# Two h units moved between the first columns, five relus split over two engines, one more tile's y from mixed blocks

## The chip, the cores and the metric

The kernel runs on one core of a Trainium2 chip. The metric is the device time of one execution in microseconds (us), and the median of several executions is quoted. The profile's span, from the first to the last instruction, is about 1.8 us shorter than the time.

The TensorE multiplies matrices and writes to PSUM. VectorE (DVE), ScalarE (ACT) and GpSimd (POOL) do the elementwise work.

## The reference

```python
# u, v: 8 x 3008 x 256; z: 8 x 3008 x 64; w_in: 256 x 2048; w_out: 2048 x 256
scores = np.matmul(z, z.transpose(0, 2, 1)) / 3008
attn = np.maximum(scores, 0.0) ** 2
x = (u * np.matmul(attn, v)).reshape(24064, 256)
h = x @ w_in
g = h * np.cos(h)
y = g @ w_out
```

## The kernel before

The tokens are cut into 48 tiles of up to 512 tokens, six to a batch. Attention is done per tile ("column" of the score matrix). A score group is two 128 x 512 blocks of scores; ScalarE takes the relu, VectorE the square. A column's two output halves (`dh` 0 and 1) gather in two pairs of PSUM banks: the pair `M`, and a pair taken from the three double-bank buffers `E`, which also hold scores and h.

```python
    def emit_score(later=None):
        ...
        r = rpool.tile([P, 2, CW], FP16, name="r")
        nc.scalar.activation(r[:, :, 0:W], e[:, :, 0:W], AF.Relu)
        def square():
            ...
                nc.vector.tensor_tensor(a4, r[:, :, 0:W], r[:, :, 0:W], ALU.mult)
```

At a column's end both pairs must be emptied before the next column may write them. ScalarE copies one bank of a pair, VectorE adds the other:

```python
    def gate_sum(s, b0, b1):
        W = width(s % NC)
        sm = spool.tile([P, CW], FP32, name="sm")
        nc.scalar.copy(sm[:, 0:W], b0[:, 0:W])
        nc.vector.tensor_tensor(sm[:, 0:W], b1[:, 0:W], sm[:, 0:W], ALU.add)
        return sm
```

In columns 0 to 2 no other work is placed that could fill a gap. Key pieces (four steps of 128 keys each) serve one output half and then the other:

```python
    def phase_a_first(s, n, extra={}):
        ...
        acc = [pair, M] if s == 1 else [M, pair]
        last = NB - 1
        steps = [
            (dh, k)
            for I in range(NC)
            for dh in range(2)
            for k in range(4 * I, min(4 * I + 4, last))
        ] + [(2, last)]
        ...
        late_sums.extend(gate_sum(s, *acc[dh]) for dh in range(2))
        hold(late_sums[0][0:1, 0:1])       # POOL waits here for VectorE's sum
        ...
    phase_a_first(0, 12, {4: lambda: turn_late(4), 8: lambda: turn_late(5)})
    phase_a_first(1, 12)
    nc.gpsimd.dma_start(w_out16, moe_w_out.rearrange("(k p) f -> p k f", p=P))
    phase_a_first(2, 14)
    ...
    phase_b(2)
```

An h unit is 4 matmuls of 512 columns into one `E` buffer (8 in a row in a timeline are two units), a cosine on ScalarE, and the product h x cos(h) on VectorE. `phase_b(2)` works off the eight units of tile 0 and the eight of tile 1, with the y of tile 0 between them in eight pieces:

```python
        if s == 2:
            hs = [(0, i) for i in range(8)] + hs
        ...
        if n > 8:
            after = (1, 3, 5, 7, 9, 11, 13, 14)
```

For tiles 1 to 45 y is made from seven products of mixed (added and subtracted) blocks in place of eight; the mixing is done by POOL and VectorE. Tiles 0, 46 and 47 are multiplied directly.

Of the kernel before, what the change touches and what calls it, by code (L numbers as in the profile page):

```python
# [14 lines left out]
def kernel(  # L15
# [9 lines left out]
    nc = tc.nc  # L25
    AF = mybir.ActivationFunctionType
    ALU = mybir.AluOpType
# [151 lines left out]
    turn_slots = {}  # L179
    done_groups = [0]  # L180

    def emit_score(later=None):
        b, J, I, h = groups[done_groups[0]]
        done_groups[0] += 1
        cut = I == J and not (b == 0 and J < 3)
        W = 2 * P if cut and h == 0 else width(J)
        zT = zTs[b]
        e = E[take_e()]
        for t in range(2):
            k = 4 * I + 2 * h + t  # L190
            half = t if h == 0 else 1 - t
            rows = slice(half * H, (half + 1) * H)
            Wt = min(W, (2 * h + t + 1) * P) if cut else W
            nc.tensor.matmul(  # L194
                e[:, t, 0:Wt],
                zT[rows, k * P:(k + 1) * P],
                zT[rows, J * CW:J * CW + Wt],
                start=True,
                stop=True,
            )  # L200
        key = (b, J, I)
        a = new_piece(key) if h == 0 else piece(key)
        r = rpool.tile([P, 2, CW], FP16, name="r")
        nc.scalar.activation(r[:, :, 0:W], e[:, :, 0:W], AF.Relu)  # L204
        def square():
            if I > J:
                a4 = a.rearrange("p (k t j) -> p t k j", k=4, j=P)[:, 2 * h:2 * h + 2, :, :]
                r4 = r.rearrange("p t (k j) -> p t k j", j=P)
                nc.vector.tensor_tensor(a4, r4, r4, ALU.mult)  # L209
            else:  # L210
                a4 = a.rearrange("p (k w) -> p k w", w=CW)[:, 2 * h:2 * h + 2, 0:W]
                nc.vector.tensor_tensor(a4, r[:, :, 0:W], r[:, :, 0:W], ALU.mult)  # L212

        if later is None:
            square()
        else:
            later.append(square)
        if h == 0:
            return
        if cut or (I > J and (b, J, I) not in direct):  # L220
            turns.append(((b, I), key))
            turns.sort(key=lambda t: t[0])
            turn_slots[key] = pieces[key]
            pending[pieces[key]] = "held"
# [122 lines left out]
    def phase_a_first(s, n, extra={}):  # L347
        b, J = s // NC, s % NC
        ea = e_order.pop(0)
        pair = [E[ea][:, 0, :], E[ea][:, 1, :]]  # L350
        acc = [pair, M] if s == 1 else [M, pair]
        last = NB - 1
        steps = [
            (dh, k)
            for I in range(NC)
            for dh in range(2)
            for k in range(4 * I, min(4 * I + 4, last))
        ] + [(2, last)]
        lo, hi = 5 if s == 0 else 2, 42
        at = {}  # L360
        for i in range(n):
            p = lo + (hi - lo) * i // (n - 1)
            at[p] = at.get(p, 0) + 1
        for i, (dh, k) in enumerate(steps):
            if i in extra:
                extra[i]()
            if dh == 2:
                emit_value(b, J, last, 0, 0, acc[0][0], False, True)
                emit_value(b, J, last, 1, 1, acc[1][1], False, True)
            else:  # L370
                for t in range(2):
                    emit_value(
                        b, J, k, t, dh, acc[dh][t], k == 0, k == last - 1 and t != dh
                    )
            if dh > 0 and (k % 4 == 3):
                drop_piece((b, J, k // 4))
                if s > 0:
                    emit_turns((0, 0), 1)
                    if k < 4:
                        turn_u(s)  # L380
                    elif k < 8:
                        for d in range(2):
                            gate_mul(s - 1, d, late_sums.pop(0))
            for _ in range(at.get(i, 0)):
                emit_score(later=squares if s == 0 and i == lo else None)
        if s == 0:
            turn_u(0)
        late_sums.extend(gate_sum(s, *acc[dh]) for dh in range(2))
        hold(late_sums[0][0:1, 0:1])
        load_u(s + 1)  # L390
        e_order.append(ea)
# [24 lines left out]
        )  # L416

    def mixed(m):
        return 1 <= m < NSLOT - 2

    F = NFT // 2
    T = 2 * P
# [38 lines left out]
            )  # L461
        nc.scalar.activation(y_outs[m][0][:, 1, :], acc, AF.Copy, bias=0.0, scale=inv_s2)

    def product(m, n):
        g = gs[m]
        nk, up, low = halves_of(m)
        nk = nk // P
        t = lambda i: w_mix[:, i, :, :]
        left, right = {
            1: (g[:, 0:F, up], w_out16[:, 0:F, 0:P]),  # L470
            2: (g[:, F:, up], w_out16[:, F:, 0:P]),
            3: (s4, w_out16[:, F:, P:D]),
            4: (g[:, F:, low], t(3)),
            5: (s1, t(0)),
            6: (s2, t(1)),
            7: (g[:, 0:F, low], t(2)),
        }[n]
        at = order_y.index(n) + (nk == 1 and n in order_y[4:])
        acc = M[at % 2][:, 0:nk * P]
        for ft in range(F):  # L480
            for k in range(nk):
                nc.tensor.matmul(  # L482
                    acc[:, k * P:(k + 1) * P],
                    left[:, ft, k * P:(k + 1) * P],
                    right[:, ft, :],
                    start=(ft == 0 and k == 0),
                    stop=(ft == F - 1 and k == nk - 1),
                )
        acc = acc.rearrange("p (k d) -> p k d", d=P)
        if n == 5:  # L490
            y_outs[m] = [opool.tile([P, 2, D], FP32, name="o") for i in range(2)]
            y_parts[m] = {}
        c11, c12, c21, c22 = (y_outs[m][i][:, 0:nk, d * P:(d + 1) * P] for i in range(2) for d in range(2))
        parts = y_parts[m]
        add = lambda dst, other: nc.vector.scalar_tensor_tensor(
            dst, acc, inv_s2, other, ALU.mult, ALU.add
        )
        if n in (1, 5, 6):
            parts[n] = ypool.tile([P, 2, P], FP32, name=f"p{n}")[:, 0:nk, :]
        if n in (1, 5):  # L500
            nc.scalar.activation(parts[n], acc, AF.Copy, bias=0.0, scale=inv_s2)
        elif n == 6:
            add(parts[6], parts[1])
            nc.gpsimd.tensor_tensor(c12, parts[6], parts[5], ALU.add)
        elif n == 7:
            add(c21, parts[6])
            nc.gpsimd.tensor_tensor(c22, c21, parts[5], ALU.add)
        elif n == 2:
            add(c11, parts[1])
        elif n == 3:  # L510
            add(c12, c12)
            store_half(m, 0, y_outs[m][0])
        else:
            add(c21, c21)
            store_half(m, 1, y_outs[m][1])

    def y_bank(m, k):
        if m == NSLOT - 1 and k == 3:
            return E[0][:, 0, 0:D]
        return M[k // 2][:, (k % 2) * D:(k % 2 + 1) * D]  # L520

    def y_block(m, ft, k):
        final = m == NSLOT - 1
# [58 lines left out]
    def phase_b(s):  # L582
        y, hs = s - 2, [(s - 1, i) for i in (0, 4, 1, 5, 2, 6, 3, 7)]
        if s == 2:
            hs = [(0, i) for i in range(8)] + hs
        for dh in range(len(late_sums)):
            gate_mul(s, 2 - len(late_sums), late_sums.pop(0), nc.gpsimd)
        if mixed(y):
            ys = [lambda n=n: product(y, n) for n in order_y]
            if mwidth(y) < CW:  # L590
                ys.insert(4, lambda: middle(y))
        else:
            ys = [lambda i=i: emit_y(y, i) for i in range(8)]
            ys[7] = lambda f=ys[7]: (f(), store_y(y))
        n = len(hs)
        if n > 8:
            after = (1, 3, 5, 7, 9, 11, 13, 14)
        elif mixed(y):
            after = (0, 1, 2, 3, 4, 5, 6, 6)
        else:  # L600
            after = (0, 1, 2, 3, 4, 5, 6, 6)
        for i, (m, unit) in enumerate(hs):
            times_c = emit_h(m, unit)
            if not mixed(y):
                times_c()
            for f, place in zip(ys, after):
                if place == i:
                    f()
            if mixed(y):
                times_c()  # L610
            if mixed(m) and unit >= 4:
                mix_early(m, unit - 4)
            if i in (1, 3, 5):
                emit_turns((0, 0), 1)
# [52 lines left out]
    emit_score(later=squares)  # L667
    emit_score(later=squares)
    turn_on_pe(2)
    copy_turned(2)  # L670
    squares.pop(0)()
    squares.pop(0)()
    M = [ppool.tile([P, CW], FP32, name=f"M{i}", tag=f"M{i}") for i in range(2)]

# [25 lines left out]
    phase_a_first(0, 12, {4: lambda: turn_late(4), 8: lambda: turn_late(5)})  # L700
    phase_a_first(1, 12)
    nc.gpsimd.dma_start(w_out16, moe_w_out.rearrange("(k p) f -> p k f", p=P))
    phase_a_first(2, 14)
    assert done_groups[0] == need[3]
    emit_turns((0, 3))
# [63 lines left out]
```

## Time and profile before

| what | value |
|---|---|
| time | 1197.2 us (1196.8 to 1197.6 in 3 runs) |
| span of the profiled run | 1194.3 us |
| TensorE busy | 1184.6 us, 99% |
| first score of column 0 | 5.46 us |
| first h of tile 0 / first y of tile 0 | 52.05 / 55.52 us |
| column 3 begins / h of tile 2 begins | 74.70 / 86.33 us |
| h of tile 47 begins / last y's `E` bank begins | 1168.92 / 1188.06 us |

The landmarks are first starts on the TensorE's timeline. They cut the span into a start that is full of waits (to 86.33 us), a steady part (up to tile 47) and a last stage (to the last `E` bank). The TensorE waits nowhere in the steady part. Of the page's 40 slices, of 30 us each, only the second and the last are below 90% busy; the second row is the granted clock:

```profile
PE   9899999999999999999999999999999999999998
...
PEclk9999999999999999999999999999999999999999
```

### The profile page before, as it was taken

Reading aid. Unit: us, or ns where it says so; the run is one execution under the profiler, and the core shown is the slowest. Engines: PE = TensorE matmul, PEld = TensorE weight load, DVE = VectorE, ACT = ScalarE, POOL = GpSimd, SP = SyncE. Lnnn points to the kernel's source line nnn. Section 1 sums busy time; section 2 is a strip of 40 time slices with the busy share of each in tenths; the row PEclk is TensorE's granted clock in tenths of the full one; section 3 lists DMA queues with packets and bytes.
Section 4 is the critical chain, followed back from the end, with each engine's and each line's share of the span. In section 5 each row is a group of like instructions: output and inputs, shape, how many; then the busy total and the mean of one; then the engine's idle time right before and its main releaser. Section 6 shows DMA issues by size and latency. Waiting matters only on the chain.

```text
span 1194.3 us, 28924 instructions
## 1 busy us (share of the span) xinstructions
PE 1184.6 (99%) x11839; PEld 727.2 (61%) x11839; DVE 1008.6 (84%) x1293; ACT 795.1 (67%) x927; POOL 678.4 (57%) x707
## 2 busy tenths in 40 slices
PE   9899999999999999999999999999999999999998
PEld 4556655665566656566556665666656666665566
DVE  6798988888988898888988889888888888888775
ACT  7866666666766676666766676766766666666454
POOL 3186745557565573665647556476565765545450
PEclk9999999999999999999999999999999999999999
DMA  9999898769995699956999459974798838954301
GB/s 159 172 165 163 121 153 127 118 107 137 139 139 104 114 140 157 128 92 113 150 147 132 91 107 156 169 117 77 121 160 154 122 70 122 183 105 89 65 19 54
DMA packets 479861, 147.98 MB, mean 124 GB/s; under 512 B 404208, under 2 KB 479472, under 8 KB 479728
## 3 DMA queue, kind: packets, MB, share of 16 engines
q1 hardware_dynamic: 380752, 112.93, 54.5%
q0 software_dynamic: 97440, 32.78, 28.1%
q8 instruction: 92, 1.51, 0.5%
q10 hardware_dynamic: 1536, 0.43, 0.2%
q14 instruction: 41, 0.34, 0.1%
HBM read 66.32 MB, written 24.64 MB: 76 GB/s over the span
## 4 chain that ended last, share of the span: by engine, by line
PE 97%; ACT 1%; DVE 1%; issue 1%; ACTq 0%; DVEq 0%
PE E L403 27%; PE M L482 23%; PE M L258 20%; PE E L258 19%; PE E L194 5%; PE M L524 2%; ACT r L204 1%; PE M L459 1%; PE E L654 0%; DVE sm L270 0%; PE E L524 0%; DVE A L209 0%; DVE x L286 0%; DVE g L414 0%; PE M L677 0%
## 5 line engine op out<-in xcount | busy, mean ns | idle before, releaser
L411 ACT ACTIVATE c<-E 128x1024 f16<-128x1024 f32 (+1 forms) x384 | 385.6, 1006 | 218.0 <-PE E L403 214.8
L414 DVE SCALAR_TENSOR_TENSOR g<-E,c 128x1024 f16<-128x1024 f32 (+1 forms) x384 | 458.9, 1197 | 66.7 <-ACT c L411 65.7
L204 ACT ACTIVATE r<-E 128x512 f16<-128x512 f32 (+1 forms) x342 | 327.8, 967 | 114.1 <-PE E L194 108.4
L258 PEld LDWEIGHTS <-v 64*128 64x128 f16 x4512 | 246.8, 94 | 232.4 <-issue 20.6
L403 PE MATMUL E<-x,w_in 128*128 128x512 f16 (+1 forms) x1408 | 353.8, 375 | 0.0
L432 POOL TENSOR_TENSOR s<-g 128x512 f16<-128x512 f16 (+1 forms) x180 | 202.9, 1127 | 185.4 <-DVE g L414 138.9
L258 PE MATMUL M<-A,v 64*128 64x512 f16 (+1 forms) x2256 | 284.9, 372 | 2.1 <-ACT sm L269 1.2
L258 PE MATMUL E<-A,v 64*128 64x512 f16 (+1 forms) x2256 | 279.4, 372 | 0.0
L433 POOL TENSOR_TENSOR g<-g 128x512 f16<-128x512 f16 (+1 forms) x180 | 214.2, 1190 | 14.1
L403 PEld LDWEIGHTS <-w_in 128*128 128x128 f16 x1536 | 133.4, 98 | 108.6 <-issue 19.1
L482 PEld LDWEIGHTS <-g 128*128 128x128 f16 x2752 | 168.6, 98 | 39.8
L209 DVE TENSOR_TENSOR A<-r 128x1024 f16<-128x1024 f16 x240 | 173.3, 734 | 15.1 <-ACT r L204 14.3
L286 POOL TENSOR_TENSOR x<-sm,uT 128x512 f16<-128x512 f32 (+1 forms) x43 | 48.5, 1130 | 214.1 <-DVE sm L270 213.9
L482 PEld LDWEIGHTS <-s 128*128 128x128 f16 x2064 | 126.6, 98 | 30.6
L194 PE MATMUL E<-zT 64*128 64x512 f16 (+4 forms) x684 | 130.0, 356 | 0.5 <-ACT zT L647 0.3
L439 DVE TENSOR_TENSOR s<-s,g 128x1024 f16<-128x1024 f16 (+1 forms) x90 | 98.5, 1094 | 2.1 <-POOL s L432 2.1
L482 PE MATMUL M<-w_out,g 128*128 128x128 f16 x1376 | 91.5, 219 | 0.0
L482 PE MATMUL M<-w_mix,g 128*128 128x128 f16 x1376 | 91.5, 219 | 0.0
L482 PE MATMUL M<-w_mix,s 128*128 128x128 f16 x1376 | 91.5, 219 | 0.0
L212 DVE TENSOR_TENSOR A<-r 128x512 f16<-128x512 f16 (+1 forms) x102 | 80.7, 792 | 10.2 <-ACT r L204 9.4
L194 PEld LDWEIGHTS <-zT 64*128 64x128 f16 x684 | 39.3, 94 | 36.7 <-issue 2.2
L441 DVE TENSOR_TENSOR s<-g,s 128x1024 f16<-128x1024 f16 (+1 forms) x90 | 59.4, 662 | 0.0
(58 smaller groups left out, 657.6 us busy)
## 6 DMA issues: line engine op xcount, KB each, us to landing
out_dram<-o SPq DMA_DIRECT2D x87, 256.0 KB, 2.2
v<-in_v_dram POOLq DMA_DIRECT2D x40, 256.0 KB, 9.2
u<-in_u_dram POOLq DMA_DIRECT2D x40, 256.0 KB, 4.8
A<-A SPq DMA_TRANSPOSE x252, 5.2
z<-in_z_dram POOLq DMA_DIRECT2D x14, 192.0 KB, 10.6
z<-in_z_dram POOLq DMA_DIRECT2D x14, 176.0 KB, 6.3
v<-in_v_dram POOLq DMA_DIRECT2D x8, 192.0 KB, 12.0
u<-in_u_dram POOLq DMA_DIRECT2D x8, 192.0 KB, 4.0
```

The costliest lines, as they stand in the source:

```text
L194: nc.tensor.matmul(e[:, t, 0:Wt], zT[rows, k * P:(k + 1) * P], zT[rows, J * CW:J * CW + Wt], start=True, stop=True,)
L204: nc.scalar.activation(r[:, :, 0:W], e[:, :, 0:W], AF.Relu)
L209: nc.vector.tensor_tensor(a4, r4, r4, ALU.mult)
L212: nc.vector.tensor_tensor(a4, r[:, :, 0:W], r[:, :, 0:W], ALU.mult)
L258: nc.tensor.matmul(bank[:, 0:width(J)], vs[b, k // 4][t * H:(t + 1) * H, k % 4, dh * P:(dh + 1) * P], value_rhs(b, J, k, t), start=start, ...
L403: nc.tensor.matmul(e[:, f, 0:W], w_in16[:, k, ft * P:(ft + 1) * P], x[:, k, 0:W], start=(k == 0), stop=(k == 1),)
L411: nc.scalar.activation(c[:, :, 0:W], e[:, :, 0:W], AF.Sin, bias=half_pi, scale=inv_s2)
L414: return lambda: nc.vector.scalar_tensor_tensor(gs[m][:, 2 * i:2 * i + 2, 0:W], e[:, :, 0:W], 1.0, c[:, :, 0:W], ALU.mult, ALU.mult)
L432: nc.gpsimd.tensor_tensor(s1[:, f, 0:n], g[:, f, low], g[:, lower, low], ALU.add)
L433: nc.gpsimd.tensor_tensor(g[:, f, low], g[:, f, up], g[:, f, low], ALU.subtract)
L439: nc.vector.tensor_tensor(s2[:, f, 0:n], s1[:, f, 0:n], g[:, f, up], ALU.subtract)
L482: nc.tensor.matmul(acc[:, k * P:(k + 1) * P], left[:, ft, k * P:(k + 1) * P], right[:, ft, :], start=(ft == 0 and k == 0), stop=(ft == F - ...
```

## The change

The author wants to close the TensorE's gaps at the start, and to save a little at the end, in four parts.

1. **Piece order.** In columns 1 and 2 each output half takes two key pieces at a time, so the second pair of banks is needed 8 steps after the column's start and not 4.
2. **Moved h units.** Two h units of tile 0 fill the gap between columns 1 and 2. Fourteen units remain after column 2, and the pieces of y move forward among them.
3. **Tile 46** gets its y from mixed blocks; tile 47 uses the `M` banks in the other order.
4. **Shared relus.** In groups 0, 14, 15, 26 and 27 (the first, and the last two of columns 0 and 1) ScalarE takes one half of the relu and VectorE the other. Group 0's square is also done in two halves, and earlier.

```diff
+    shared_groups = {0, 14, 15, 26, 27}
...
-        nc.scalar.activation(r[:, :, 0:W], e[:, :, 0:W], AF.Relu)
+        shared = done in shared_groups
+        n = 1 if shared else 2
+        nc.scalar.activation(r[:, 0:n, 0:W], e[:, 0:n, 0:W], AF.Relu)
+        if shared:
+            nc.vector.tensor_scalar(r[:, 1, 0:W], e[:, 1, 0:W], 0.0, None, ALU.max)
...
+        run = 1 if s == 0 else 2
...
-            for I in range(NC)
+            for I in range(0, NC, run)
             for dh in range(2)
-            for k in range(4 * I, min(4 * I + 4, last))
+            for k in range(4 * I, min(4 * (I + run), last))
...
-        return 1 <= m < NSLOT - 2
+        return 1 <= m < NSLOT - 1
...
-            hs = [(0, i) for i in range(8)] + hs
+            hs = [(0, i) for i in range(2, 8)] + hs
...
-            ys = [lambda n=n: product(y, n) for n in order_y]
+            late = s == NSLOT
+            ys = [
+                lambda n=n, i=i: product(y, n, i)
+                for i, n in enumerate((1, 5) + order_y[2:] if late else order_y)
+            ]
...
-            after = (1, 3, 5, 7, 9, 11, 13, 14)
+            after = (1, 2, 4, 5, 7, 8, 10, 11)
+        elif s == NSLOT:
+            after = (0, 1, 3, 4, 5, 6, 7)
...
+            if s == NSLOT and i in (1, 3):
+                for c in range(2):
+                    mix_late(y, "s2" if i == 1 else "s4", c)
...
     nc.gpsimd.dma_start(w_out16, moe_w_out.rearrange("(k p) f -> p k f", p=P))
+    for i in range(2):
+        emit_h(0, i)()
     phase_a_first(2, 14)
```

More of the change, by code (lines that the diff above doesn't have):

```diff
@@ L180 @@
     done_groups = [0]
+    shared_groups = {0, 14, 15, 26, 27}
     def emit_score(later=None):
-        b, J, I, h = groups[done_groups[0]]
+        done = done_groups[0]
+        b, J, I, h = groups[done]
         done_groups[0] += 1
@@ L208, in square @@
                 r4 = r.rearrange("p t (k j) -> p t k j", j=P)
-                nc.vector.tensor_tensor(a4, r4, r4, ALU.mult)
             else:
                 a4 = a.rearrange("p (k w) -> p k w", w=CW)[:, 2 * h:2 * h + 2, 0:W]
-                nc.vector.tensor_tensor(a4, r[:, :, 0:W], r[:, :, 0:W], ALU.mult)
+                r4 = r[:, :, 0:W]
+            parts = [slice(0, 1), slice(1, 2)] if done == 0 else [slice(0, 2)]
+            for t in parts:
+                nc.vector.tensor_tensor(a4[:, t], r4[:, t], r4[:, t], ALU.mult)
         if later is None:
@@ L462, in middle, with product @@
         nc.scalar.activation(y_outs[m][0][:, 1, :], acc, AF.Copy, bias=0.0, scale=inv_s2)
-    def product(m, n):
+    def product(m, n, place):
         g = gs[m]
@@ L477, in product @@
         }[n]
-        at = order_y.index(n) + (nk == 1 and n in order_y[4:])
-        acc = M[at % 2][:, 0:nk * P]
+        acc = M[(place + (nk == 1 and place >= 4)) % 2][:, 0:nk * P]
         for ft in range(F):
@@ L489, in product @@
         acc = acc.rearrange("p (k d) -> p k d", d=P)
-        if n == 5:
+        if m not in y_outs:
             y_outs[m] = [opool.tile([P, 2, D], FP32, name="o") for i in range(2)]
@@ L519, in y_bank @@
             return E[0][:, 0, 0:D]
-        return M[k // 2][:, (k % 2) * D:(k % 2 + 1) * D]
+        bank = 1 - k // 2 if m == NSLOT - 1 else k // 2
+        return M[bank][:, (k % 2) * D:(k % 2 + 1) * D]
     def y_block(m, ft, k):
@@ L669 @@
     turn_on_pe(2)
+    squares.pop(0)()
     copy_turned(2)
-    squares.pop(0)()
     squares.pop(0)()
```

## The prediction

> **What bounds the kernel now.** I read the page first (shares and slices), then the waits of the TensorE, then its timeline around those waits, then the timelines of the two engines that ended them, and last the chain that ended last, over the final 20 us.
>
> ```profile
> PE 1184.6 (99%) x11839; PEld 727.2 (61%) x11839; DVE 1008.6 (84%) x1293; ACT 795.1 (67%) x927; POOL 678.4 (57%) x707
> ...
> PE M L524 <- DVE g L414: 1.6, 1, 1.6
> PE M L258 <- ACT sm L269: 1.2, 1, 1.2
> ...
> PE M L258 <- DVE sm L270: 0.9, 2, 0.6
> ```
>
> The TensorE is busy for 1184.6 of 1194.3 us. Its whole list of waits comes to about 5 us, and the timeline puts all of it in the first 56 us: from there to 1190 us it streams without a gap. So the kernel is TensorE-bound, and a change can win only by taking matmul time away or by closing those early gaps. Here are the gaps on the TensorE's timeline.
>
> ```profile
> 23.82 0.38 PE L258 MATMUL M<-A,v 64*128 64x512 f16 x1
> 24.47 0.59 PE L258 MATMUL M<-A,v 64*128 64x512 f16 x3 [0.28 <-DVE sm L270]
> ...
> 36.09 0.38 PE L258 MATMUL E<-A,v 64*128 64x512 f16 x1
> 37.69 0.37 PE L258 MATMUL M<-A,v 64*128 64x512 f16 x1 [1.22 <-ACT sm L269]
> 38.65 0.80 PE L258 MATMUL M<-A,v 64*128 64x512 f16 x5 [0.59 <-DVE sm L270]
> ...
> 52.05 1.90 PE L403 MATMUL E<-x,w_in 128*128 128x512 f16 x8
> 55.52 1.05 PE L524 MATMUL M<-w_out,g 128*128 128x256 f16 x8 [1.58 <-DVE g L414]
> ```
>
> Columns: start, length, engine, line, operation, and in brackets the idle time and what ended it. The printed length of a lone matmul includes its drain (0.38), so I count slots instead: a 512-column matmul, or a pair of half-height ones, takes 0.216 us start to start (16 half-height ones took 1.73 us in the chain). By slots the three gaps are:
> - between columns 0 and 1: 23.82 + 0.216 to 24.47, 0.43 us;
> - between columns 1 and 2: 36.09 + 0.22 to 38.65, less the one matmul in it, 2.1 us;
> - between column 2 and the first tile's y: 52.05 + 8 x 0.216 = 53.78 to 55.52, 1.74 us.
>
> The second gap is a bank pair, M, that ScalarE (copy) and VectorE (sum) must have read before the next column may write it. VectorE does this back to back:
>
> ```profile
> 36.70 0.69 DVE L212 TENSOR_TENSOR A<-r 128x1024 f16<-128x1024 f16 x1 [0.38 <-ACT r L204]
> 37.31 0.68 DVE L270 TENSOR_TENSOR sm<-E,sm 128x512 f32<-128x512 f32 x1
> 37.91 0.68 DVE L270 TENSOR_TENSOR sm<-M,sm 128x512 f32<-128x512 f32 x1
> ```
>
> **What the Trainium skill says.** (1) "VectorE: DVE Perf Modes", section "Why PSUM operands drop a tier": a PSUM operand in fp32 runs at one element per cycle whatever the operation. So a relu of 512 fp32 columns on VectorE costs as much as the two sums above: 0.68 us, next start after 0.60 us. The trace agrees on the sums (512 columns in 0.68 us, 1024 in 1.22 us); no relu on VectorE has run yet. (2) "PSUM — Partial Sum Buffer", section "Specifications (TRN2)": ScalarE and VectorE can read PSUM in parallel when they are in different banks. The two halves of a score tile are 512 fp32 columns each, one bank each, so the shared relu is legal; no run here shows it yet. (3) "TensorE: Matmul & The Clock Gate", section "Wait — 56ns, not 53.3ns?": warm matmuls start 55.6 ns (128 columns) and 215.7 ns (512 columns) apart. The trace agrees: 16 of 128 columns take 0.89 us, 8 of 512 take 1.73 us.
>
> **The change part by part.**
>
> *Moved h units.* Two of the first tile's eight h units (8 matmuls, 1.73 us) move from after column 2 into the second gap. Their x is ready: the gating products ran at 29.2 to 30.5 us. Their weights too: w_in was issued at 14.0 us and landed 11.2 us later. They remove no work, they fill a gap. In the third gap the y of tile 0 then needs VectorE products made long before, not 54.24 to 55.48 us.
>
> *What they collide with.* Each unit also brings a ScalarE cosine (1.0 us) and a VectorE product (1.22 us, next start 1.13), and holds a score buffer until the product has read it. Working through VectorE in program order from the square that starts at 34.60: square to 35.2, half relu to 35.8, square to 36.4, half relu to 37.0, square to 37.6, sum of E to 38.2, sum of M to 38.9, products to 40.0 and 41.2. The TensorE ends column 1 at 36.31, does the h units to 38.04, then waits for M until 38.9, for the first score buffer until 40.0 (it stood at 39.09 in the kernel before) and for the second until 41.2. So it reaches the third score of column 2 near 42.1, against 40.82 before: the 1.73 us are nearly all given back for the moment.
>
> *The credit comes in the third gap.* Column 2 then ends near 53.5 instead of 52.05, but only 12 units follow the first y instead of 14. Two h units fill 53.5 to 55.2, and y of tile 0 can start at about 55.3. That is not free: w_out decides it. It is issued at 39.31 and lands 16.0 us later:
>
> ```profile
> L702 POOL DMA_DIRECT2D w_out<-in_moe_w_out_dram x1: 1159/1159/1159, 39.3 to 39.3; - x1
> ...
> DMA to landing us min/median/max: 16.0/16.0/16.0
> ```
>
> 39.31 + 16.0 = 55.3 us, 0.2 us before its use now. The reader is to see that the wait charged to VectorE hides a transfer that comes only just earlier. From 55.3, 12 units of 0.865 and 8 pieces of y of 0.87 take 17.35 us: the stage ends at 72.65, against 74.77 (the last h of the stage ends there in the chain). Gain 2.1 us.
>
> *Two key pieces per output half, columns 1 and 2.* No matmul is added or removed; the second half of the accumulators is needed 8 steps after the start instead of 4, 0.86 us later. By itself that closes the first gap (0.43 us).
>
> *Shared relus.* Groups 14, 15 and 26, 27 are the last two of columns 0 and 1. ScalarE saves 0.4 us on each (1.02 against 0.60 for 512 columns). But its copy of M starts at 22.99 because the TensorE ended then, and its copy of E at 36.56 likewise, so little is won; VectorE gets 0.60 us more for each, and VectorE has the last word on both banks. At the first seam its sum of E ends near 25.5 instead of 25.02, and the score at 25.07 needs that buffer. I book -0.4 us there, which takes back what the piece order wins. Group 0: four filler matmuls stand in front of the first value matmul anyway; below 0.1 us.
>
> *y of tile 46.* 64 matmuls of 256 columns (8 in 0.87 us: 7.0 us) become 7 products of 16 matmuls of 128 columns (0.89 us each: 6.23 us). That is 0.77 us less for the TensorE. VectorE pays: its 8 products at 1.13, 5 additions at 0.34 and 4 mixing operations at 0.61 make 13.2 us in a stage in which the TensorE now has 8 x 0.865 + 6.23 = 13.15 us. Before, it had 8 x 1.13 = 9 us in 13.9 us:
>
> ```profile
> 1168.22 1.73 PE E L403 x8
> ...
> 1182.98 5.24 PE M L524 x48
> ```
>
> Following both engines by hand, product 6 waits about 0.4 us for the first mix, and the last y starts some 13.7 us after the stage's start instead of 13.9. Gain 0.2 us; the tail after it (4 stores) is as before.
>
> **The sum:** 2.1 + 0.2 + under 0.1 = 2.3 us; 1197.2 - 2.3 = 1194.9 us.
>
> **The rivals.** (a) All gaps close: 0.43 + 2.1 + 1.74 + 0.77 = 5.0 us, 1192.2 us. For it: the four parts aim at exactly these places. Against it: VectorE's list above, and w_out at 55.3 us. (b) The score buffers held by the h units, with VectorE's extra relus, cost as much as the gap: no gain at the start and only the 0.2 us at the end, 1197.0 us. For it: the TensorE is even with the kernel before at 42 us. Against it: the two units need not be done later, and the third gap is 1.74 us of pure waiting. (c) The last stage becomes VectorE-bound, with POOL's mixing slowing it (squares at 77 to 83 us took up to 1.64 us beside POOL instead of 0.69), and loses 0.5 to 1 us: 1195.7 us. (d) w_out lands later, as more transposes compete with it: each us costs a us.
>
> **Range and chances.** From (a) at one end and (b) at the other I take 1193.3 to 1196.8 as eight in ten. A change by 2% is 24 us; all waits and removed work together are 5 us, so within 2% is all but certain (0.985). I leave 0.005 for faster and 0.01 for slower, the latter for an unforeseen stall that repeats in every tile; nothing in the steady tiles changes order.
>
> **What would show it.** Right: the gap between columns 1 and 2 holds 8 matmuls of h; then waits of the TensorE for M (about 0.9 us) and for score buffers that VectorE's h products hold (about 1.2 us); the first y near 55.3 us with w_out or nothing as its releaser; the stage's end near 72.7 us; 7 products beside the h of the last tile, with a short wait for the s2 mix; VectorE near fully busy there. Wrong: y of tile 0 starting well before 55 us (then rival a), the stage ending at 74 us or later (b), the last y starting more than 14.2 us after its stage's start (c), or a new TensorE wait between 75 and 1165 us.

## The result

The changed kernel takes 1194.81 us (1194.51 to 1196.36 in 4 runs), the kernel before 1197.01 us (4 runs in all). All ratios below are the mean time of one kernel's fast runs over that of the other's of the same rounds, so they are not quite the ratio of the medians. Here the ratio is 0.9984, with a 95% interval of 0.9966 to 1.0001: within 2%, and on these runs alone not clear of no change.

The TensorE's list of waits in the profile after (line, who ended the wait, total us, times, longest; three entries of the warm-up and the first scores, 1.2, 0.3 and 0.2 us, which the kernel before has too, are cut):

```profile
PE E L197 <- DVE sm L280: 0.9, 1, 0.9
PE M L268 <- DVE sm L280: 0.6, 1, 0.6
PE E L197 <- DVE r L211: 0.5, 2, 0.3
PE M L268 <- DVE A L222: 0.4, 1, 0.4
PE E L197 <- DVE g L425: 0.3, 1, 0.3
PE M L492 <- POOL s L443: 0.3, 1, 0.3
```

The waits of 1.6 us (for VectorE's h product) and 1.2 us (for ScalarE's copy) are gone. In their place stand smaller ones: the first five hang on VectorE, the sixth is at the end, in tile 46. These are the places on the TensorE's timeline after (start, length, work, and in brackets the idle time and its releaser):

```profile
24.25 0.39 PE L197 MATMUL E<-zT 64*128 64x512 f16 x2 [0.31 <-DVE r L211]
24.47 0.82 PE L268 MATMUL E<-A,v 64*128 64x512 f16 x6
26.18 0.39 PE L197 MATMUL E<-zT 64*128 64x512 f16 x2 [0.89 <-DVE sm L280]
...
37.51 1.90 PE L414 MATMUL E<-x,w_in 128*128 128x512 f16 x8
39.34 0.39 PE L268 MATMUL M<-A,v 64*128 64x512 f16 x1
40.30 0.80 PE L268 MATMUL M<-A,v 64*128 64x512 f16 x5 [0.57 <-DVE sm L280]
...
54.44 1.90 PE L414 MATMUL E<-x,w_in 128*128 128x512 f16 x8
56.31 1.05 PE L535 MATMUL M<-w_out,g 128*128 128x256 f16 x8
```

At 37.51 the two h units fill the old gap between columns 1 and 2. At 54.44 two more lead straight into the first y. But the second score of column 1 starts at 26.18, where the kernel before had it at 25.07, and what it waits for is VectorE's sum. That engine's timeline there:

```profile
22.19 0.68 DVE L211 TENSOR_SCALAR r<-E 128x512 f16<-128x512 f32 x1
22.91 0.69 DVE L222 TENSOR_TENSOR A<-r 128x1024 f16<-128x1024 f16 x1
23.51 0.68 DVE L211 TENSOR_SCALAR r<-E 128x512 f16<-128x512 f32 x1
24.23 0.69 DVE L222 TENSOR_TENSOR A<-r 128x1024 f16<-128x1024 f16 x1
24.84 0.68 DVE L280 TENSOR_TENSOR sm<-M,sm 128x512 f32<-128x512 f32 x1
25.44 0.68 DVE L280 TENSOR_TENSOR sm<-E,sm 128x512 f32<-128x512 f32 x1
```

VectorE works without a pause, the two half relus (L211) stand in front of the sums (L280), and the sum that frees `E` ends at 26.12 us.

The landmarks, with the start of the first score taken off where noted, since that start itself scatters from 5.36 to 5.76 us between profiled runs:

| us | before | after |
|---|---|---|
| first score | 5.46 | 5.37 |
| first score to second score of column 1 | 19.61 | 20.81 |
| first y of tile 0 begins | 55.52 | 56.31 |
| column 3 begins | 74.70 | 73.76 |
| length of column 3 | 11.63 | 11.23 |
| h of tile 2 begins | 86.33 | 84.99 |
| h of tile 2 to h of tile 47 | 1082.59 | 1082.59 |
| h of tile 47 to last `E` bank | 19.14 | 19.08 |
| span | 1194.3 | 1192.9 |

The two profiled runs took 1196.1 and 1194.72 us, so the profile before is of a run 0.9 us faster than its median. The gain in span of 1.4 us is made as follows: the first y starts 0.8 us later, two h units less follow (1.73 us), column 3 is 0.4 us shorter, the last stage 0.06 us. The steady part is the same to 0.01 us.

### The profile page after: what moved, and what is told of

It reads as the page before. It is cut to its first block, busy times and chain, and to the rows that moved or that the text cites. A ratio compares the mean times of both kernels' runs of the same rounds, so it can differ in the third digit from the quotient of the medians.

```text
span 1192.9 us, 29048 instructions
## 1 busy us (share of the span) xinstructions
PE 1183.7 (99%) x11887; PEld 725.8 (61%) x11887; DVE 1015.5 (85%) x1308; ACT 793.1 (66%) x927; POOL 689.7 (58%) x717
## 4 chain that ended last, share of the span: by engine, by line
PE 97%; DVE 1%; ACT 1%; issue 0%; POOL 0%; DVEq 0%; ACTq 0%
PE E L414 27%; PE M L492 23%; PE M L268 20%; PE E L268 19%; PE E L197 5%; PE M L535 1%; ACT r L209 1%; PE M L470 1%; DVE A L222 0%; DVE g L425 0%; DVE r L211 0%; PE E L674 0%; DVE sm L280 0%; PE E L535 0%; POOL s L443 0%
## 5 line engine op out<-in xcount | busy, mean ns | idle before, releaser
L443 POOL TENSOR_TENSOR s<-g 128x512 f16<-128x512 f16 (+1 forms) x184 | 208.0, 1131 | 188.6 <-DVE g L425 138.7
L222 DVE TENSOR_TENSOR A<-r 128x1024 f16<-128x1024 f16 (+2 forms) x343 | 253.3, 750 | 22.5 <-ACT r L209 21.0
L444 POOL TENSOR_TENSOR g<-g 128x512 f16<-128x512 f16 (+1 forms) x184 | 219.3, 1192 | 14.4
L492 PEld LDWEIGHTS <-g 128*128 128x128 f16 x2816 | 172.5, 98 | 40.8
L492 PEld LDWEIGHTS <-s 128*128 128x128 f16 x2112 | 129.4, 98 | 32.0 <-DVE s L450 0.5
L197 PE MATMUL E<-zT 64*128 64x512 f16 (+4 forms) x684 | 127.5, 355 | 2.3 <-DVE sm L280 0.9
L492 PE MATMUL M<-w_mix,s 128*128 128x128 f16 x1408 | 94.0, 219 | 0.3 <-POOL s L443 0.3
L197 PEld LDWEIGHTS <-zT 64*128 64x128 f16 x684 | 38.8, 94 | 39.3 <-issue 4.7
L279 ACT COPY sm<-E 128x512 f32<-128x512 f32 (+1 forms) x48 | 27.7, 577 | 42.0 <-PE E L268 42.0
```

The costliest lines, as they stand in the source:

```text
L197: nc.tensor.matmul(e[:, t, 0:Wt], zT[rows, k * P:(k + 1) * P], zT[rows, J * CW:J * CW + Wt], start=True, stop=True,)
L222: nc.vector.tensor_tensor(a4[:, t], r4[:, t], r4[:, t], ALU.mult)
L443: nc.gpsimd.tensor_tensor(s1[:, f, 0:n], g[:, f, low], g[:, lower, low], ALU.add)
L444: nc.gpsimd.tensor_tensor(g[:, f, low], g[:, f, up], g[:, f, low], ALU.subtract)
L492: nc.tensor.matmul(acc[:, k * P:(k + 1) * P], left[:, ft, k * P:(k + 1) * P], right[:, ft, :], start=(ft == 0 and k == 0), stop=(ft == F - ...
```

## The experiments

The theory: the moved units bring more than the whole gain, and the shared relus, by holding up VectorE's sums, give part of it back; w_out's landing is a second limit on the first y. The rivals: the gain comes from the piece order or from tile 46; the sharing costs nothing because w_out decides alone.

Twelve kernels ran, in three lots of four, each lot on one chip with its own runs of the kernel before (medians 1196.53, 1196.47 and 1197.44 us, n = 9 each). All were right against the reference. In the table "start" runs from the first score to tile 2's first h, in the profiled run; the last two columns are lengths of the steady part and of the last stage.

| kernel | median us | ratio to before [95%] | start | steady | last stage |
|---|---|---|---|---|---|
| before | | | 80.87 | 1082.59 | 19.14 |
| after | 1194.81 | 0.9984 [0.9966, 1.0001] | 79.62 | 1082.59 | 19.08 |
| e1_after_again | 1195.02 | 0.9984 [0.9972, 0.9997] | 79.34 | 1082.59 | 19.08 |
| e2_no_share | 1193.41 | 0.9974 [0.9961, 0.9986] | 78.69 | 1083.23 | 19.08 |
| e3_no_move | 1199.03 | 1.0018 [1.0004, 1.0031] | 82.10 | 1082.60 | 19.08 |
| e4_no_mix | 1194.96 | 0.9986 [0.9973, 0.9998] | 80.01 | 1082.59 | 19.13 |
| e5_run_one | 1194.86 | 0.9985 [0.9973, 0.9998] | 79.13 | 1082.60 | 19.08 |
| e6_share_first | 1194.32 | 0.9981 [0.9969, 0.9994] | 80.11 | 1082.85 | 19.08 |
| e7_w_out_early | 1192.93 | 0.9968 [0.9955, 0.9980] | 77.61 | 1082.60 | 19.08 |
| e8_other_order | 1195.19 | 0.9985 [0.9971, 0.9999] | 79.19 | 1082.84 | 18.55 |
| e9_y_last | 1194.24 | 0.9974 [0.9961, 0.9986] | 78.87 | 1082.60 | 19.09 |
| e10_sums_first | 1192.38 | 0.9957 [0.9943, 0.9970] | 77.00 | 1083.34 | 19.08 |
| e11_best | 1191.97 | 0.9957 [0.9944, 0.9969] | 77.43 | 1083.25 | 18.54 |
| e12_share_w_out_early | 1194.69 | 0.9976 [0.9963, 0.9988] | 79.38 | 1082.60 | 19.08 |

### e1_after_again

The changed kernel, unaltered.

> The changed kernel once more, unchanged, as the yardstick for the other runs of this batch. Expected 1194.8 us, within 0.5 us, ratio to the kernel before 0.998; in the profile the first y near 56.3 us, column 3 from 73.8 us, last y from 1181.4 us.

The ratio is again 0.9984, now with an interval that leaves out 1. Its start differs from the first profile's by 0.28 us; a difference of that size in one profile means nothing by itself.

### e2_no_share

```diff
-    shared_groups = {0, 14, 15, 26, 27}
+    shared_groups = set()
-            parts = [slice(0, 1), slice(1, 2)] if done == 0 else [slice(0, 2)]
+            parts = [slice(0, 2)]
-    squares.pop(0)()
     copy_turned(2)
+    squares.pop(0)()
```

> The changed kernel with no shared relu at all (and the first square whole, in its old place). My theory: the shared relus cost time, because VectorE gets 0.6 us more for each and has the last word on the buffers that the TensorE waits for. Then the first wait of 0.4 us at 9.6 us goes, the score that starts at 26.2 us starts near 25.1, the first y near 55.3 and the total falls by about 1 us. The rival, the change's own intent: ScalarE is relieved, and without sharing the total rises by 0.3 to 0.5 us.

By the medians it is 1.6 us faster than e1; by the two ratios, 0.0010 x 1197, 1.2 us. So the shared relus cost time (the edit also takes out group 0's halved, earlier square). Three lines of its TensorE timeline:

```profile
25.27 0.39 PE L197 MATMUL E<-zT 64*128 64x512 f16 x2 [0.66 <-DVE sm L280]
...
55.67 1.05 PE L535 MATMUL M<-w_out,g 128*128 128x256 f16 x8 [0.69 <-DMA w_out<-in_moe_w_out_dram]
...
98.25 1.47 PE L268 MATMUL M<-A,v 64*128 64x512 f16 x12 [0.57 <-DVE o L505]
```

From the last score of column 0 to the second of column 1 it takes 3.43 us, as in the kernel before (21.64 to 25.07), against 4.15 us in e1 and in the first profile after (22.03 to 26.18). So at this first seam (between columns 0 and 1) the sharing costs 0.72 us. The order of pieces brings nothing there: without sharing it is 3.43 us with the new order (e2) as with the old (before). Column 2 then ends so early that the first y waits 0.69 us for w_out: the second limit is now the first one. And column 4 has a new wait of 0.57 us, which the section on what stays open takes up. The profiled run was the slowest of the five (1194.75 us).

### e3_no_move

```diff
-            hs = [(0, i) for i in range(2, 8)] + hs
+            hs = [(0, i) for i in range(8)] + hs
-            after = (1, 2, 4, 5, 7, 8, 10, 11)
+            after = (1, 3, 5, 7, 9, 11, 13, 14)
-    for i in range(2):
-        emit_h(0, i)()
```

> The changed kernel with all eight h units of tile 0 after column 2 again (and the y pieces placed as in the kernel before). My theory: the moved units are what wins. Without them the gap between columns 1 and 2 and the one before the first y are empty again: first y near 57 us with 14 units to follow, column 3 from about 76.5, total up by 2.5 us. The rival, that the moved units give back what they fill since they hold two score buffers: total up by 0.3 us at most.

Without the move, the other three parts make the kernel slower than before: the start is 1.2 us longer (82.10 against 80.87). The ratio says so too (1.0018, interval above 1), but see below for its clock. The old gaps are back, and the second is wider than it was (1.14 in place of 0.59 us), because VectorE comes later to its sum of `M`:

```profile
40.14 0.80 PE L268 MATMUL M<-A,v 64*128 64x512 f16 x5 [1.14 <-DVE sm L280]
...
57.02 1.05 PE L535 MATMUL M<-w_out,g 128*128 128x256 f16 x8 [1.57 <-DVE g L425]
```

The start is 2.5 to 2.8 us longer than in the two profiles of the changed kernel. By the medians the loss is 4.0 us, but three of the five runs had a clock of 0.998 and took 1199.0 to 1199.7 us; the two at 1.000 took 1197.5 us, 2.5 us above e1. I take 2.5 to 2.8 us. Of this, 0.4 us is column 3 (11.63 us, against 11.23 in the changed kernel), since the edit puts the pieces of y back as well; up to column 3 the moved units alone are worth 2.1 to 2.4 us. Why the clock was granted lower in three runs isn't known.

### e4_no_mix

```diff
-        return 1 <= m < NSLOT - 1
+        return 1 <= m < NSLOT - 2
```

(With tile 47's banks, the places and the late mixes as before.)

> The changed kernel with y of tile 46 direct, as in the kernel before. My theory: the mixed form saves 0.77 us of matmul time, but waits for POOL and VectorE return nearly all of it, so undoing it costs 0.0 to 0.2 us; the stage from the first h of tile 47 to the last y takes 13.9 us instead of 13.84. The rival: the saving counts in full and undoing it costs 0.7 us.

The times are those of e1 within what can be told apart (in its profile the first y waits 0.73 us for w_out, hence the longer start). The last stage says it exactly: 19.13 in place of 19.08 us. Tile 46's part of the change is worth 0.05 us.

### e5_run_one

```diff
-        run = 1 if s == 0 else 2
+        run = 1
```

> The changed kernel with one key piece per output half in columns 1 and 2, as before the change. My theory after the profile: the order of pieces decides nothing, since the score that waits for VectorE's sum of E (26.2 us) and, two columns on, the score buffers held by the h products end last either way; total within 0.3 us of the changed kernel (ratio to the kernel before 0.998), score in column 1 still near 26.2 us. The rival, the change's intent: M is needed 0.86 us sooner and the first gap of 0.43 us comes back, total up by 0.4 us or more.

The old piece order costs nothing: 0.9985, and a start no longer than with the new order. Its timeline has the same interval filled differently:

```profile
25.62 0.59 PE L268 MATMUL M<-A,v 64*128 64x512 f16 x3 [0.52 <-DVE sm L280]
26.22 0.39 PE L197 MATMUL E<-zT 64*128 64x512 f16 x2
```

The value matmuls wait for `M` again, but the score after them starts at 26.22 us, 20.46 us after the first score, against 20.14 to 20.81 us in the six profiles with the new order and all the sharing. From column 0's last score it is 4.15 us, with either order. VectorE sums `E` right after `M`, here from 25.48 to 26.16 us, so the score couldn't have started earlier in any case: the wait for `M` lies inside the wait for `E`.

### e6_share_first

```diff
-    shared_groups = {0, 14, 15, 26, 27}
+    shared_groups = {0}
```

> The changed kernel with the relu shared for group 0 alone (groups 14, 15, 26, 27 on ScalarE again). Theory: of the 1.1 us that sharing costs by the end of column 1, 0.4 us are group 0 (wait of the second half of the first value matmuls at 9.6 us) and 0.7 us the seams. So the wait of about 0.4 us at 9.6 us stays, the score in column 1 starts near 25.5 us, and the total lies between the changed kernel and the one without sharing: 0.5 to 1.0 us below the changed kernel. The rival, that group 0's sharing is the part that helps: total equal to or below the kernel without sharing, ratio 0.997 or less.

The five times are 1193.4 (twice), 1194.3 and 1195.9 us (twice). The profiled run is one of the slowest, and its waits show why; the others have no profile:

```profile
PE M L535 <- DMA w_out<-in_moe_w_out_dram: 1.8, 1, 1.8
```

w_out landed 17.2 us after its issue, at 57.1 us. So the total can't tell what group 0 is worth. The timeline shows that the seam is as without sharing: 3.43 us from the last score of column 0 to the second of column 1. What group 0 costs it can't tell. The stretch before, from the first score to the last of column 0, is 15.99 to 16.66 us in the eight profiles that share group 0 and 15.96 to 16.39 in the six that don't; the means are 0.2 us apart, and the ranges overlap. The wait of 0.4 us at 9.6 us that was expected to stay isn't in e6's list, and in e1's neither.

### e7_w_out_early

e2, and the load of w_out issued before column 1:

```diff
+    nc.gpsimd.dma_start(w_out16, moe_w_out.rearrange("(k p) f -> p k f", p=P))
     phase_a_first(1, 12)
-    nc.gpsimd.dma_start(w_out16, moe_w_out.rearrange("(k p) f -> p k f", p=P))
```

> The kernel without sharing, with the load of w_out issued one column earlier (before column 1 instead of after it). Theory: without sharing, the first y waits for the transfer of w_out (0.7 us in the profile); issued at about 25 us it lands before 45 us, the first y starts near 54.9 instead of 55.7 us. Whether the total falls by as much is open: in the profile without sharing column 4 waited 0.6 us for POOL, which had waited for the turned z until 85.8 us. If that wall stays, the total is the same as without sharing (ratio 0.997); if the lighter queue moves the wall too, it falls by 0.5 to 0.8 us (0.9965). The rival, that w_out is not what the first y waits for: first y still at 55.7 us.

It takes 1192.93 us, and its five runs lie within 0.8 us. w_out is issued at 25.4 us and lands 11.7 us later, and the first y follows the h units without a wait:

```profile
52.76 1.90 PE L414 MATMUL E<-x,w_in 128*128 128x512 f16 x8
54.49 1.04 PE L535 MATMUL M<-w_out,g 128*128 128x256 f16 x8
```

### e12_share_w_out_early

The changed kernel with all its sharing, and the load of w_out moved as in e7 and nothing else.

> The changed kernel with its sharing and with the early load of w_out alone. Against the kernel without sharing and with the early load (1192.9 us) it gives the cost of sharing with no wait for w_out in either. Theory: 1.1 us, as the start of the waiting score in column 1 shows, so 1194.0 us, first y near 55.7 us with no wait for w_out. The rival, that w_out and not sharing is what the earlier runs showed: 1193.0 us.

```profile
26.40 0.39 PE L197 MATMUL E<-zT 64*128 64x512 f16 x2 [0.89 <-DVE sm L280]
...
54.67 1.90 PE L414 MATMUL E<-x,w_in 128*128 128x512 f16 x8
56.41 1.04 PE L535 MATMUL M<-w_out,g 128*128 128x256 f16 x8
```

w_out, on the chip since 38.6 us (26.8 + 11.8), bounds nothing here, and the first y still comes at 56.41 us. So in the first profile after it is column 2's end that sets the first y, and w_out's landing hides just behind it. In e1, e8 and e4 w_out came later still, and the first y waited 0.2, 0.2 and 0.7 us for it. Against e7, which differs only in part 4 (the sharing and group 0's square), the start is 1.8 us longer (79.38 and 77.61): 0.6 us of it before the first seam, where profiles scatter (see e6), and 1.2 us at the two seams. The ratios differ by 0.0008, 1.0 us, but come from two chips.

### e8_other_order

```diff
-                for i, n in enumerate((1, 5) + order_y[2:] if late else order_y)
+                for i, n in enumerate((1, 2, 5, 6, 7, 3, 4) if late else order_y)
```

> The changed kernel with the products of the last but one tile in the order 1, 2, 5, 6, 7, 3, 4 instead of 1, 5, 6, 7, 2, 3, 4: the second product that needs no mixing comes ahead of those that do. Theory: the 0.3 us wait for POOL's last s1 and the 0.2 us wait for s2 are what is left of the 0.77 us saved; with them hidden the stage from the first h of tile 47 to the last y falls from 13.84 to about 13.3 us and the total by 0.4 to 0.5 us. The rival, that VectorE with some 13.2 us of work bounds this stage: 13.8 us as now, total unchanged.

Tile 46's products in this order need POOL's mix later. The last stage falls from 19.08 to 18.55 us. That is 0.58 us less than with direct y (19.13, e4), of the 0.77 us that the fewer matmuls can give. In the total this is not seen: 0.9985, and 0.9985 too for e5, which differs from the changed kernel by the piece order alone. In the profile 0.25 us of it was lost in the steady part (0.18 of them in a wait of column 4); the rest is within the scatter of the totals.

### e9_y_last

e7, and the pieces of y later:

```diff
-            after = (1, 2, 4, 5, 7, 8, 10, 11)
+            after = (1, 3, 5, 7, 9, 11, 12, 13)
```

> The kernel without sharing and with the early load of w_out, with the y pieces of tile 0 placed so that the last one comes directly ahead of column 3 (after units 1, 3, 5, 7, 9, 11, 12, 13 instead of 1, 2, 4, 5, 7, 8, 10, 11). Theory: in the kernel before, column 3 took 11.63 us instead of 11.23, because its banks are those that ScalarE still copies y out of; the change's new places hide these copies under two h units. So column 3 takes about 11.6 us again and the total rises by 0.4 us, to about 1193.3. The rival, that the places do not matter: total unchanged at 1192.9.

```profile
72.53 1.94 PE L268 MATMUL M<-A,v 64*128 64x512 f16 x12 [0.73 <-ACT o L565]
```

Column 3 waits 0.73 us for ScalarE to copy y out of `M`, and then takes 11.70 us in place of 11.22 (e7). The start is 1.3 us longer than e7's. In the changed kernel the same copies lie beside two h units: that is the 0.4 us by which its column 3 is shorter. (e3, with the old places, has 11.63 us again; the eleven profiles with the new ones have 11.22 or 11.23.) In the kernel before the copies ran from 73.99 to 75.07 us, while column 3 began at 74.70.

### e10_sums_first

e7, and VectorE sums the pair `E` first after columns 0 and 1:

```diff
-        late_sums.extend(gate_sum(s, *acc[dh]) for dh in range(2))
+        sums = {dh: gate_sum(s, *acc[dh]) for dh in ((1, 0) if s < 2 else (0, 1))}
+        late_sums.extend(sums[dh] for dh in range(2))
```

> The kernel without sharing and with the early load of w_out, with the two sums after columns 0 and 1 swapped: the accumulator pair that the next stage needs first is read first. Theory: the order of VectorE's last instructions sets the start of the waiting score in column 1; it starts 0.6 us sooner (24.4 instead of about 25.0), and the total falls by 0.4 to 0.6 us, to about 1192.4. The rival, that another wait takes its place at once: total unchanged.

```profile
24.48 0.39 PE L197 MATMUL E<-zT 64*128 64x512 f16 x2
...
96.69 1.47 PE L268 MATMUL M<-A,v 64*128 64x512 f16 x12 [0.66 <-DVE o L506]
```

The second score no longer waits. From the last score of column 0 it takes 2.83 us, here and in e11, against 3.43 us in every other profile that doesn't share groups 14 and 15: the sum of `E` was what it had waited for. The start shortens by 0.6 us against e7's (by 0.2 us in e11, whose first 16 us were slower); column 4 takes 0.66 us back in this run, the slowest of its five. Its ratio is below e12's (0.9957 and 0.9976); the intervals overlap, but its slowest run (1193.17 us) is faster than e12's fastest (1194.24).

### e11_best

e10 with the order of e8.

> All that the experiments point to: moved units and mixed y of tile 46 as in the change, no sharing, early load of w_out, sums swapped, product order 1, 2, 5, 6, 7, 3, 4. Theory: the previous one less 0.5 us in the last stage: about 1191.8 us, ratio 0.996 to the kernel before. If the last stage does not count, 1192.4.

It takes 1191.97 us, at a ratio of 0.9957: 5.1 us under the kernel before, 2.7 us under e12. The changed kernel: at 1194.81 us it is 2.8 us above. It was run at another time. So a version with no shared relu, an early w_out and two reorderings beats both kernels.

### What stays open: the start of column 4

In e2, e8, e10 and e11 column 4 waits for VectorE's additions to tile 1's y. Those wait for POOL, and POOL had stood waiting for the transposes of the next batch's z before it could issue loads. From e2's POOL timeline:

```profile
85.81 1.14 POOL L118 DMA_DIRECT2D z<-in_z_dram  x1 [3.52 <-DMA zT<-z]
```

From this start to column 4's it is 12.44 us in e2 (85.81 to 98.25), e10 (84.25 to 96.69) and e11 (84.58 to 97.02), and 12.43 in e8. In the changed kernel the two stand at 85.80 and 98.26, so it reaches column 4 just as this limit would begin to bind; in e7 (83.89, 96.43) it does not bind. The release of POOL varies from 81.97 (e9) to 87.76 us (e3) between profiled runs, and I found nothing that explains it. I read it as a further limit for anything that starts earlier, and as one reason why totals of the faster kernels scatter. No run moved that z or its loads, so this is argued from timelines and not tested.

## Why the prediction was right

The time came out at 1194.81 us against 1194.9 us. That they agree to 0.1 us is in part luck: the gain was foreseen at 2.3 us and is 2.2 us by the medians, but 1.9 us by the ratio, 1.5 us in e1's lot and 1.4 us in the profiles. Most of the mechanism was right; some sizes were not, and in part they cancelled.

- **The bound.** Right: the steady part did not change by more than 0.01 us, and all that was won lies in the start and the last stage.
- **The moved units.** Right in kind: 8 matmuls of h in the gap, then a wait for `M` (0.57 us; about 0.9 foreseen), then scores behind VectorE's h products (0.33 us; about 1.2 foreseen). The part was booked at 2.1 us for the stage; e3 puts it at 2.1 to 2.4 us up to column 3, so this term was right.
- **The shared relus.** This is the term that was mis-sized. It was booked at -0.4 us at the first seam, to be made good by the piece order. The two seams cost 0.72 and 0.45 us, each the same to 0.02 us from profile to profile: to the second score of column 1 it is 4.15 in place of 3.43 us (see e2), and from there to the two h units before the first y 28.26 in place of 27.81 us. That makes 1.2 us, as by the totals of e1 and e2 (1.2 us; e12 and e7 give 1.0). The half relus stand before VectorE's sums, so that they put off the very sum for which the TensorE then waits. What was missed besides is that the two halves did not run side by side. In no shared group of the profile after does VectorE's half start before ScalarE's has ended; in group 0 the wait for it is in all eight profiles that share it (why VectorE waits there, no run shows):

```profile
6.43 0.69 DVE L211 TENSOR_SCALAR r<-E 128x512 f16<-128x512 f32 x1 [0.81 <-ACT r L209]
```

ScalarE's half ran from 5.80 to 6.40 us. So the relu took 1.3 us in place of the 1.02 us of ScalarE alone. Group 0 was booked below 0.1 us; what it costs can't be told from the scatter (e6). Rival (b) had VectorE's extra relus as its cause, but took it to eat the whole gain.

- **The piece order.** Wrong: it does not close the first gap. The second score can't start before VectorE's sum of `E`, 0.6 us after that of `M`; closing the wait for `M` only uncovers the wait for `E` (e5, and e2 against the kernel before). So nothing made good the booked 0.4 us, and the first seam lost 0.72 us where none was to be lost. Summing `E` first removes it (e10).
- **VectorE's list in the second gap.** Right in its order, late by 1.3 us as a whole: the sum of `M` was to end at 38.9 us and ended at 40.25. That is the 1.2 us by which the second score of column 1 is late in this profile, carried on (0.72 us of it from the seam).
- **The first y.** Foreseen at 55.3 us with w_out as the limit, measured at 56.31. w_out was issued at 41.0 and not 39.3 us, since POOL's issue waits for a sum of VectorE that also came late, and landed at 56.3. But column 2's end alone allowed only 54.44 + 1.73 = 56.17 us. The two limits lay within 0.15 us of each other in this profile. In e12 w_out is removed as a limit and the start is no shorter than e1's (79.38 and 79.34 us); in e7, with both removed, it is 1.7 to 2.0 us shorter than in the two profiles of the changed kernel. Rival (d), a later landing, is what e6's profiled run shows.
- **The end of the stage.** Foreseen at 72.65 us, measured at 73.76, which by the prediction's own test lay close to (b). So 1.1 of the 2.1 us booked for the stage were missing. 0.4 us were made good by something that the prediction did not have: column 3 became that much shorter, as the copies of y moved off its start (e9).
- **Tile 46.** Booked at 0.2 us, measured at 0.06 (0.05 in e4). By slots the TensorE idles 0.49 us in product 5, for POOL's mix, and 0.17 us in product 6; the prediction had 0.4 us at product 6 alone. The wait is in the second line below. e8's order removes it.

```profile
1170.20 0.83 PE L492 MATMUL M<-w_mix,s 128*128 128x128 f16 x12
1171.36 0.40 PE L492 MATMUL M<-w_mix,s 128*128 128x128 f16 x4 [0.32 <-POOL s L443]
```

- **The rest of the sum.** In the starts, 2.5 to 2.8 us won by the move and the new places of y less 1.2 to 1.8 us for the sharing leaves 0.7 to 1.6 us; the two profiles of the changed kernel show 1.25 and 1.53 us against before.
- **The skill.** "VectorE: DVE Perf Modes", section "Why PSUM operands drop a tier", held: the half relu, which had not run before, took 0.68 us, as much as the sums. The shared reading of one tile's two banks gave right results in every run, but no trace here shows the two engines reading them at the same time.

## What to carry to other kernels

When the TensorE waits at a seam between two stages, list what the engine that has the last word must still do, and take work off it; halving a task between two engines lengthens the list of the one that ends the wait, and here the halves did not even overlap. Independent matmuls put into such a gap pay off later, at the place where they need not be done any more, so follow the credit to that place and ask what else (a landing, a copy) starts there at nearly the same time. A part whose worth is below the scatter of totals, like the 0.05 us of tile 46, can still be read from the landmarks of its own stage. Count a landmark from the nearest one before it: from the first score the first seam scattered by 0.7 us between like profiles, from the last score before it by 0.01 us.

## What the Trainium skill lacked or had wrong

- "TensorE: Matmul & The Clock Gate", section "Back-to-back issue gap", gives for a stream of weight load and matmul pairs about 131 ns at 512 columns and 81 ns at 128. Here, where every matmul has its own weight load, 8 of 512 columns take 1.74 us (54.67 to 56.41 in e12), 217 ns each, and 16 of 128 columns 0.89 us, 56 ns each. The formula which that section calls the isolated gap is the one that fits.
- "DMA: Bandwidth & Descriptors", section "Anatomy of one DMA — SWDGE (gpsimd) path", fits a POOL-issued load by 2.0 us plus its bytes at 436 GB/s. For w_out's 2.1 MB in fp32 that is an estimate of 6.8 us. The same load landed 11.7 us (e7), 15.3 us (after) and 17.2 us (e6) after its issue. The page gives no figure for how far a load stretches beside other transfers, and the first y hung on it. Whether other transfers are the reason, no run here shows.
- "SBUF — State Buffer", section "🔬 SBUF: two separate sides", says that a VectorE operation with two SBUF inputs and a GpSimd operation that reads SBUF take turns on a shared port pair. The trace before agrees: squares of 1024 fp16 columns took 1.64 us beside POOL's additions and 0.69 us alone. The page gives no size for this pair of operations to plan with.
- No page has that work started on a column of half-height matmuls while one of its banks is still being read costs time beyond the wait. In e9 the column was 0.48 us longer after its 0.73 us wait. In the kernel before and in e3 it was 0.4 us longer without a listed wait. Why is open.
